# A Fourier-mixing layer with a gated MLP: x added by accumulating stores, three weight pairs split earlier, and the first two units of each MLP2 block interleaved

## The chip, the cores and the metric

The kernel runs on one core of one Trainium2 chip. The metric is the device time of one execution in microseconds (us). Several executions of the same program are timed, and their median is given. Beside that stands one execution that a profiler recorded; its rows are what the profile shows. Engines are named as in the profile: PE is the matrix engine (TensorE), DVE the vector engine, ACT the scalar engine, POOL is GpSimd, and SP is the engine that mainly issues transfers.

## What is computed

For x of 2048 tokens by 512 features, all in float32:

```python
xn = layernorm(x)                       # over the 512 features
a = xn @ dft_hid_re.T;  b = xn @ dft_hid_im.T
s = dft_seq_re @ a - dft_seq_im @ b     # real part of the 2D Fourier transform
h = relu(xn @ w1 + b1) ** 2             # w1: 512 x 1792
g = silu(h @ w2 + b2)                   # w2: 1792 x 512
out = x + s * g
```

## The kernel before, in words

**Arithmetic.** Every float32 operand is split into a high part (ACT, L69) and a low part (DVE, L72), both of type float32r, and each product of two operands is made of three passes: high x high, high x low, low x high. On top of that, products of 2 x 2 blocks are made by the Strassen-Winograd scheme with seven products instead of eight. So each operand first needs four *sums* (`sums_a`, `sums_b`, on DVE), and its seven pieces are then split. The seven results are put together by `combine` (L234): one copy by ACT and four DVE operations (L240 to L243) that read the PSUM banks.

**Stages.** (1) The sequence transform comes first, in eight blocks c of 256 columns with eight steps j each. Blocks 0 and 1 are computed plainly, blocks 2 to 7 by Strassen-Winograd (`mm`, L300). For each step a raw tile of the DFT matrix (`r`, 512 KB, L190, three slots) is loaded, its sums are formed (`t`, two slots) and it is split into two sets of moving operands, two steps ahead of use. `stage2` (L287) multiplies the result by the hidden-dimension DFT matrices and stores s as `Y` in memory. During this stage DVE and ACT also prepare the weight pairs (`make_w`): all seven of w1, and of w2 those that are not made later; they are stored in memory as `W1D` and `W2D`.
(2) MLP1 (`hidden`, L526) has 28 *units*, one for each of four token blocks c and seven weight pairs p, n = 7c + p. A unit is 42 matmuls. Its result is combined, goes through ReLU and square on ACT, and is stored in memory (`HD`, L558) by a transfer that ACT issues. The tile for it (`room`, L522) is one of three `r` slots or a fourth one, by n % 4.
(3) MLP2 has 28 units in the same numbering. Unit n reads `HD` back (`operand`, L561): load (SP, L570), sums (DVE, L207 to L209), split (ACT L69, DVE L72) into one of three places of `block`. A unit is 42 matmuls (`outer`, L599), which add up over the seven pairs of a block in seven PSUM regions. Before a block's first products, ACT writes the bias b2 into three of these regions (`bias`, L592). At a block's end `combine` yields z, and `finish` (L622) makes silu(z) * s + x quarter by quarter, spread over units of the next block. Silu is ACT (L640), the product is DVE (`times`, L644), and the addition of x is either DVE (`plus`, L649, with x loaded by `load_fin`) or, for two quarters of blocks 0 and 1, a transfer by GpSimd that adds x from memory onto z in SBUF (L632); `put` then stores those quarters. The last block is finished by a sequence of its own (from L846), with its last three units taken product by product (`rest`).

**What sets the order.** MLP1 and MLP2 stand under `manual_schedule`: each engine runs its instructions in the order of the program text, which a Python loop writes. `go(names)` advances a named job by one step: `h5` is operand 5 (load, sums, split), `x3` a half of the tokens of a block, `m1` its mean and scale, `w6` a late weight pair (`late_w2`), `l5` the load of a prepared pair from `W2D`. In unit n of MLP2 the loop issues the matmuls, then `h{n+3}` (sums), at a block's end the combine, then `h{n+2}` (split) and `h{n+6}` (load). `plan` puts jobs beside the units of MLP1. SP, ACT and POOL issue transfers in program order too, and wait in that order: a transfer whose source or destination isn't ready holds up what is issued behind it.

**Weight pairs of w2.** W2_LATE (4, 5) are split during MLP1 and stored in W2D. W2_DIRECT (0, 1, 6) are split straight into the place that they are used from: 0 and 1 in the last third of MLP1, and 6 in the first four units of MLP2.

**Order of products.** ORDER is 1, 2, 6, 7, 5, 3, 4. A block's first unit takes FIRST, 1, 2, 6, 4, 7, 5, 3; that of the last block FIRST_LAST. Products 2, 6 are in one pair of banks (m26), 7, 5, 3 in a group of three (m753), 1 and 4 in a bank each.

Of the kernel before, what the change touches and what calls it, by code (L numbers as in the profile page):

```python
# [12 lines left out]
P = 128  # L13
# [15 lines left out]
W2_LATE, W2_DIRECT = (4, 5), (0, 1, 6)  # L29
# [22 lines left out]
FIRST = (1, 2, 6, 4, 7, 5, 3)  # L52
# [10 lines left out]
def fnet_gated_kernel(ctx, tc, x, xt, ct, wd, w1, w2, b1, b2, out):  # L63
# [30 lines left out]

    def bcast(src, n):
        return bass.AP(tensor=src.tensor, offset=src.offset, ap=[[0, P], [1, n]])
# [10 lines left out]
    for tag, n in (("g0a", 1536), ("g1a", 2048), ("g0b", 1536), ("g1b", 2048)):  # L107
        buf(tag, [P, n], f"place_{tag}")
    b1s = pool.tile([P, NF], F32, name="b1s")
# [57 lines left out]
    def sums(g):  # L167


        s = xn32[ND * g, "tile"].rearrange("p j h (b n) -> p j (h b) n", b=2)  # L170
        t = s1[g] = buf("t", [P, ND, CW], f"s1_{g}", bufs=2)
        nc.vector.tensor_tensor(t, s[:, :, 1], s[:, :, 3], op=ALU.subtract)
        nc.vector.tensor_tensor(s[:, :, 1], s[:, :, 1], s[:, :, 0], op=ALU.subtract)
        nc.vector.tensor_tensor(s[:, :, 0], t, s[:, :, 0], op=ALU.subtract)
        return nc.vector.tensor_tensor(s[:, :, 2], s[:, :, 2], s[:, :, 0], op=ALU.add)
# [10 lines left out]
    def load_c(c, j, hs=slice(0, 2)):  # L186
        if (c, j) not in raw:
            raw[c, j] = buf("r", [P, 4, CW], f"r{c}_{j}", bufs=3)
        q = slice(2 * hs.start, 2 * hs.stop)
        nc.sync.dma_start(raw[c, j][:, q], ct[c, j, :, q])  # L190
# [22 lines left out]
    def moving(key, r):  # L213

        k = "ab"[turn[0] % 2]
        turn[0] += 1
        g0 = buf(f"g0{k}", [P, 2, 3, CW], f"g0_{key}", F32R)
        g1 = buf(f"g1{k}", [P, 2, 4, CW], f"g1_{key}", F32R)
        t = buf("t", [P, 4, CW], f"t_{key}", bufs=2)
        sums_b(t, r)  # L220
        split(g0[:, HI], g0[:, LO], r[:, I11:I21 + 1])
        split(g1[:, HI], g1[:, LO], t)
        return g0, g1
# [45 lines left out]
    def stage2(c, t, tag="bc"):  # L269
# [24 lines left out]
        nc.sync.dma_start(Y[n // TC][n % TC:n % TC + P], y)  # L294
# [227 lines left out]
    def room(n, name):  # L522

        return buf("r" if n % 4 < 3 else "sx", [P, 4, 256], name, bufs=3 if n % 4 < 3 else 1)

    def hidden(n, c, p):  # L526
# [31 lines left out]
        nc.scalar.dma_start(HD[c, p], x_)  # L558
        yield

    def operand(n, c, p):  # L561

        if n % 4 in (0, 3):
            tag, bufs = (("t", 2), ("r", 3))[n % 4 // 3]
            x_ = buf(tag, [P, 4, 256], f"hr{c}_{p}", bufs=bufs)
            e = None
        else:
            e = buf("e" if n == 2 else "g1" + "ab"[n % 4 - 1], [P, 8, 256], f"hr{c}_{p}")
            x_ = e[:, 4:8]
        nc.sync.dma_start(x_, HD[c, p])  # L570
        yield
        if e is None:
            t = buf(tag, [P, 4, 256], f"hs{c}_{p}", bufs=bufs)
            parts = (slice(0, 4), t), (slice(4, 7), x_[:, 0:3])
        else:
            t = e[:, 0:4]
            parts = (slice(0, 7), e[:, 0:7]),
        sums_a(t, x_[:, C12:C12 + 1], x_[:, C11:C22 + 1], x_[:, C11], x_[:, C21])
        yield
        g = ready[c, p] = sixth(2 + n % 3, 2)  # L580
        for s, src in parts:
            split(g[:, HI, s], g[:, LO, s], src)
        yield
# [27 lines left out]
    def load_fin(c):  # L611

        fin[c] = []
        for n, src in enumerate((Y[c], x[c * TC:(c + 1) * TC])):
            for m in range(2 if n == 0 or c > NTC - 3 else 1):
# [6 lines left out]
    def finish(c, e, k):  # L622

        if len(fin[c]) > 2 + k // 2:
            silu(e, k)
            times(c, e, k)
            plus(c, e, k)
            return
        silu(e, k)
        times(c, e, k)  # L630
        z = e[:, k].rearrange("p (k e) -> p k e", e=256)
        nc.gpsimd.dma_start(z, at(x[c * TC:(c + 1) * TC], k), accum_op=ALU.add)  # L632

    def put(c, e, k):
        nc.sync.dma_start(at(out[c * TC:(c + 1) * TC], k), e[:, k].rearrange("p (k e) -> p k e", e=256))
# [31 lines left out]
    for c, j in steps:  # L667
# [11 lines left out]
        if j in (1, 2):  # L679
            stage2(c - 1, j - 1)  # L680
# [8 lines left out]
        if c == NC - 1:  # L689
# [4 lines left out]
            if j in (2, 4):  # L694
                first = xt_half(0, j // 2 - 1, lambda k: e[:, 4:8] if (j, k) == (2, "r") else
                                buf(k, [P, 4, 256], f"x{k}0", bufs=3 if k == "r" else 2))
                next(first)
            if j in (3, 6):
                list(first)
            if j > 2:  # L700
# [33 lines left out]
    for c in range(NTC - 1):  # L734
# [5 lines left out]
        else:  # L740
            plan(c, 0, [], [f"m{c + 1}", q0, q1])
# [4 lines left out]
        if c < len(W2_LATE):  # L746
            w = f"w{W2_LATE[c]}"
# [15 lines left out]
    with ordered:  # L763
        before = None
        for n, (c, p) in enumerate(units):
# [4 lines left out]
            if n == 0:  # L770
                load_w1(5)
                load_w1(6)
            if n == len(units) - 1:
# [16 lines left out]
        for n, (c, p) in enumerate(units):  # L790
# [31 lines left out]
            go(*{0: ("l5",), 1: ("w6",)}.get(n, ()))  # L822
            if not last or p < REST:
                for k in ORDER if p else FIRST_LAST if last else FIRST:
# [4 lines left out]
            go(f"h{n + 3}")  # L829
# [4 lines left out]
            if c and not last and p in (3, 4):  # L834
                put(*done, p - 1)
            go(f"h{n + 2}", *{2: ("w6",), 3: ("w6",)}.get(n, ()), f"h{n + 6}")
# [4 lines left out]
            elif c:  # L841
                for k in ((2, 3), (0,), (1,), (), (), (), ())[p] if not last else ((), (0,), (1, 2), (3,), (), (), ())[p]:
# [93 lines left out]
```

## Time and profile before

| | |
|---|---|
| median of 3 runs | 707.34 us (707.24 to 708.02) |
| the profiled execution: time, and its span | 709.52 us, 707.7 us |
| DVE busy, MLP1 from 500 to 555 us | 50.70 of 55 us |
| DVE busy, MLP2 from 596 to 630 us | 32.44 of 34 us |
| all transfers in the span | 141.09 MB, mean 199 GB/s |
| largest rate in one fortieth of the span (548 to 566 us) | 398 GB/s |
| last matmuls start, end of the span | 699.49 us, 707.7 us |

A row of a timeline gives the start and the duration in us, the engine, the line of the kernel, the operation, output and inputs, and in square brackets the idle time of the engine before it and what ended that. A row of the waits gives who waited for whom, the total in us, how often, and the longest. A row of the transfers gives the destination and source, the engine whose queue issued it (SPq, ACTq, POOLq), the count, the size and the median time in us from issue to landing. A row of the windows gives for a stretch of the span the busy time of PE, PEld, DVE, ACT and POOL, then the granted PE clock (1.00 is full), the share of the DMA engines and GB/s.

### The profile page before, as it was taken

The numbers are of one execution on the slowest core, as the hardware profiler recorded it, in microseconds if no ns is written. First come the engines' busy times: TensorE is split into PE (matmuls) and PEld (weight loads), VectorE is DVE, ScalarE is ACT, GpSimd is POOL, SyncE is SP. The second block draws the span as 40 slices with busy tenths as digits, with TensorE's granted clock in tenths as the row PEclk, the third lists the DMA queues.
The fourth block names the chain that finished last, engine by engine and source line by source line (L and its number), as shares of the span: only waits on it lengthen the run. The fifth ranks groups of instructions, "written<-read, shape, count | busy, mean of one in ns | idle before, by whom it ended". The sixth has DMA issues, their size and how long they took to land.

```text
span 707.7 us, 12794 instructions
## 1 busy us (share of the span) xinstructions
PE 687.7 (97%) x5179; PEld 648.4 (92%) x5179; DVE 584.0 (83%) x886; ACT 346.6 (49%) x475; POOL 5.2 (1%) x8
## 2 busy tenths in 40 slices
PE   8999999999999999999999999999999898999985
PEld 5778788999999999999999989899999898999985
DVE  7999654779598798797797746999999789999885
ACT  4437332444353544544453324777777745454431
POOL 0000000000000000000000000000000000101000
PEclk9999999999999999999999999999999999999998
DMA  8622441534563653835836966665627975767652
GB/s 331 219 90 90 139 144 45 207 109 146 200 219 134 237 195 123 302 116 192 280 110 240 381 266 208 209 253 208 253 121 248 398 287 198 188 206 207 234 160 79
DMA packets 55306, 141.09 MB, mean 199 GB/s; under 512 B 5072, under 2 KB 21968, under 8 KB 53968
## 3 DMA queue, kind: packets, MB, share of 16 engines
q1 hardware_dynamic: 50128, 124.56, 50.9%
q10 hardware_dynamic: 4032, 14.68, 5.2%
q0 software_dynamic: 1088, 1.05, 1.0%
q8 instruction: 40, 0.66, 0.4%
q14 instruction: 18, 0.15, 0.1%
HBM read 97.00 MB, written 43.27 MB: 198 GB/s over the span
## 4 chain that ended last, share of the span: by engine, by line
PE 73%; DVE 17%; DMA 5%; issue 2%; ACT 1%; SPq 0%; DVEq 0%; ACTq 0%
PE m_b L300 23%; PE yps L287 12%; PE hps L545 7%; PE m_b_o L599 7%; PE m_bb L300 5%; PE m_ba L300 5%; DVE block L72 4%; PE hps_b L545 4%; PE pq_b L353 3%; PE hps_ba L545 2%; DVE g L72 2%; DMA hr<-hd 2%; DMA w2raw<-in_w 1%; PE m_bc_o L599 1%; DVE bn L133 1%
## 5 line engine op out<-in xcount | busy, mean ns | idle before, releaser
L300 PE MATMUL m_b<-g,block 128*128 128x256 f32 x1080 | 129.0, 276 | 0.0
L300 PEld LDWEIGHTS m_b<-g,block 128*128 128x128 f32 x1080 | 125.5, 188 | 0.0
L69 ACT ACTIVATE g<-r 128x768 fp32r<-128x768 f32 (+2 forms) x65 | 57.3, 884 | 83.5 <-PE m_b L300 38.3
L72 DVE TENSOR_TENSOR g<-r,g 128x768 fp32r<-128x768 f32 (+2 forms) x65 | 65.4, 1007 | 35.1 <-ACT g L69 34.7
L287 PE MATMUL yps<-wd,pq 128*128 128x512 f32 (+1 forms) x414 | 92.9, 374 | 0.0
L287 PEld LDWEIGHTS yps<-wd,pq 128*128 128x128 f32 x414 | 74.8, 188 | 14.0
L72 DVE TENSOR_TENSOR g<-t,g 128x1024 fp32r<-128x1024 f32 x48 | 58.6, 1222 | 10.6 <-ACT g L69 10.6
L545 PE MATMUL hps<-xT,block 128*128 128x256 f32 x504 | 60.1, 278 | 1.6 <-DVE h L243 1.4
L545 PEld LDWEIGHTS hps<-xT,block 128*128 128x128 f32 x504 | 58.7, 188 | 2.0 <-issue 1.5
L69 ACT ACTIVATE g<-t 128x1024 fp32r<-128x1024 f32 x48 | 50.3, 1048 | 13.2 <-PE m_ba L300 6.5
L353 PE MATMUL pq_b<-g,block 128*128 128x512 f32 x180 | 47.6, 398 | 1.8 <-DVE g L72 1.7
L599 PE MATMUL m_b_o<-w,block 128*128 128x256 f32 x360 | 44.2, 279 | 4.1 <-ACT m_b_o L592 4.1
L599 PEld LDWEIGHTS m_b_o<-w,block 128*128 128x128 f32 x360 | 42.4, 188 | 4.8 <-ACT m_b_o L592 4.7
L556 ACT ACTIVATE h<-h,b1s 128x512 f32<-128x512 f32 x56 | 37.3, 715 | 17.7 <-DVE h L242 17.4
L300 PE MATMUL m_b<-g,xc 128*128 128x256 f32 x360 | 45.1, 277 | 0.0
L69 ACT ACTIVATE block<-hr 128x768 fp32r<-128x768 f32 (+1 forms) x28 | 35.5, 1268 | 18.8 <-DVE hr L209 6.0
L72 DVE TENSOR_TENSOR block<-hr,block 128x768 fp32r<-128x768 f32 (+1 forms) x28 | 41.6, 1485 | 2.3 <-ACT block L69 2.3
L353 PEld LDWEIGHTS pq_b<-g,block 128*128 128x128 f32 x180 | 33.0, 188 | 11.3 <-DVE g L72 2.4
L300 PEld LDWEIGHTS m_b<-g,xc 128*128 128x128 f32 x360 | 42.9, 188 | 0.3
L201 DVE TENSOR_TENSOR t<-r 128x512 f32<-128x512 f32 x48 | 32.8, 684 | 5.5 <-DMA r<-in_ct 5.3
L545 PE MATMUL hps_b<-xT,block 128*128 128x256 f32 x288 | 35.0, 278 | 0.0
L545 PEld LDWEIGHTS hps_b<-xT,block 128*128 128x128 f32 x288 | 33.9, 188 | 0.0
(200 smaller groups left out, 1184.2 us busy)
## 6 DMA issues: line engine op xcount, KB each, us to landing
r<-in_ct SPq DMA_DIRECT2D x63, 512.0 KB, 3.6
hd<-h ACTq DMA_DIRECT2D x28, 512.0 KB, 4.4
hr<-hd SPq DMA_DIRECT2D x28, 512.0 KB, 4.8
w1d<-w0g SPq DMA_DIRECT2D x21, 512.0 KB, 3.3
block<-w1d SPq DMA_DIRECT2D x6, 1792.0 KB, 8.8
y<-ysb SPq DMA_DIRECT2D x16, 256.0 KB, 3.1
fin<-y SPq DMA_DIRECT2D x16, 256.0 KB, 4.8
out<-z SPq DMA_DIRECT2D x15, 256.0 KB, 3.5
```

What stands on the lines that cost most here:

```text
L69: nc.scalar.activation(hi, src, AF.Copy)
L72: return nc.vector.tensor_tensor(lo, src, hi.bitcast(F32), op=ALU.subtract)
L133: nc.vector.bn_stats(bn, t[:, h])
L201: nc.vector.tensor_tensor(t[:, 0:2], r[:, 0:1].to_broadcast([P, 2, 256]), r[:, 1:3], op=ALU.add)
L287: nc.tensor.matmul(ps[:, s], PQ[c, m, k // 2][:, a_, w:w + P], WD[m, k][:, b_, s], start=n == 0, stop=n > len(todo) - 3, skip_group_check= ...
L300: nc.tensor.matmul(ps[:, d * CW:(d + 1) * CW], w[:, a_, d * P:(d + 1) * P], mv(b_), start=first and d == 0 and (a_, b_) == (HI, HI), stop= ...
L353: nc.tensor.matmul(accs[c][k], w, g[:, b_, 2 * h:2 * h + 2], start=j == 0 and h == 0 and (a_, b_) == (HI, HI), stop=j == NJ - 1 and h == 1 ...
L545: nc.tensor.matmul(product(ms, k), W1[p][a][:, a_, q * P:(q + 1) * P], xT[c, q][:, b_, b], start=share not in first, stop=q == 1 and (a_, ...
L556: nc.scalar.activation(x_[:, s], x_[:, s], AF.Relu, bias=b1s[:, f:f + 1])
L599: nc.tensor.matmul(m[:, k * 256:(k + 1) * 256], g[:, a_, a, k * P:(k + 1) * P], W2[p][:, b_, b], start=p == 0 and k == 0 and (a_, b_) == ( ...
```

## The change

- **x by accumulating stores.** During blocks 2, 3 and 4 of the first stage SP copies the first three quarters of x into `out`, memory to memory, 1 MB each, right behind a store of `Y`. For blocks 0 to 2 of MLP2 `finish` now makes silu(z) * s, and GpSimd stores it into `out` with an accumulating transfer. `plus`, `put` and the loads of x remain for the last block alone. The quarters are finished one unit apart.
- **Pairs 4, 5, 6 in MLP1.** Pair 6 is in W2_LATE. Pair 4 is split in MLP1's first unit, pair 5 where pair 4 was, pair 6 where pair 5 was. Unit 1 of MLP2 loads pair 6 from W2D.
- **Interleaving.** In blocks 0 to 2 of MLP2, PE does some products of unit 0 and of unit 1 (1 and 4; in block 0 also 2 and 6), and then the rest of unit 0 and the rest of unit 1. At a block's end and start the split `h{n+2}` is issued ahead of the combine and of the sums `h{n+3}`.
- **Four stores by GpSimd.** The results of the last four units of MLP1 (n = 24 to 27) are stored by GpSimd, not by ACT.
- **Slots.** The `r` and `t` slots are cut from two larger tiles. Operands with n % 4 = 0 take both `t` slots as one piece, those with n % 4 = 3 the `r` slots 0 and 1, and are split by one instruction on each engine where there were two.

```diff
-W2_LATE, W2_DIRECT = (4, 5), (0, 1, 6)
+W2_LATE, W2_DIRECT = (4, 5, 6), (0, 1)
...
-FIRST = (1, 2, 6, 4, 7, 5, 3)
 FIRST_LAST = (1, 2, 5, 4, 6, 7, 3)
...
+    shared, turns, kept = {}, {"t": 0, "r": 0}, set()
+    def slot(tag, n):
+        return shared[tag][:, 4 * n:4 * n + 4]
+    def turn_of(tag, keep=False):
+        while True:
+            n = turns[tag]
+            turns[tag] = (n + 1) % {"t": 2, "r": 3}[tag]
+            if (tag, n) not in kept:
+                break
+        if keep:
+            kept.add((tag, n))
+        return slot(tag, n)
...
+    shared["r"] = pool.tile([P, 12, 256], F32, name="raws")
+    shared["t"] = pool.tile([P, 8, 256], F32, name="sums")
...
-        return buf("r" if n % 4 < 3 else "sx", [P, 4, 256], name, bufs=3 if n % 4 < 3 else 1)
+        return slot("r", n % 4) if n % 4 < 3 else buf("sx", [P, 4, 256], name)
...
-        nc.scalar.dma_start(HD[c, p], x_)
+        (nc.scalar if n < 24 else nc.gpsimd).dma_start(HD[c, p], x_)
...
+        e = shared["t"] if n % 4 == 0 else shared["r"][:, 0:8] if n % 4 == 3 else \
+            buf("e" if n == 2 else "g1" + "ab"[n % 4 - 1], [P, 8, 256], f"hr{c}_{p}")
+        x_, t = e[:, 4:8], e[:, 0:4]
         nc.sync.dma_start(x_, HD[c, p])
...
-        for s, src in parts:
-            split(g[:, HI, s], g[:, LO, s], src)
+        split(g[:, HI], g[:, LO], e[:, 0:7])
...
     def finish(c, e, k):
-        if len(fin[c]) > 2 + k // 2:
-            silu(e, k)
-            times(c, e, k)
-            plus(c, e, k)
-            return
         silu(e, k)
         times(c, e, k)
         z = e[:, k].rearrange("p (k e) -> p k e", e=256)
-        nc.gpsimd.dma_start(z, at(x[c * TC:(c + 1) * TC], k), accum_op=ALU.add)
-    def put(c, e, k):
-        nc.sync.dma_start(at(out[c * TC:(c + 1) * TC], k), e[:, k].rearrange("p (k e) -> p k e", e=256))
+        nc.gpsimd.dma_start(at(out[c * TC:(c + 1) * TC], k), z, accum_op=ALU.add)
...
-            stage2(c - 1, j - 1)
+            y_stored = stage2(c - 1, j - 1)
+        if PLAIN <= c < PLAIN + NTC - 1 and j == 2:
+            part_ = slice((c - PLAIN) * TC, (c - PLAIN + 1) * TC)
+            with tc.issue_after(y_stored.ins):
+                nc.sync.dma_start(out[part_], x[part_])
...
-            plan(c, 0, [], [f"m{c + 1}", q0, q1])
+            plan(c, 0, [], [f"m{c + 1}", q0, q1] + [f"w{W2_LATE[0]}"] * 3)
...
-        if c < len(W2_LATE):
-            w = f"w{W2_LATE[c]}"
+        if c < len(W2_LATE) - 1:
+            w = f"w{W2_LATE[c + 1]}"
...
                 load_w1(6)
+                go(f"w{W2_LATE[0]}")
...
-            go(*{0: ("l5",), 1: ("w6",)}.get(n, ()))
-            if not last or p < REST:
-                for k in ORDER if p else FIRST_LAST if last else FIRST:
+            go(*{0: ("l5",), 1: ("l6",)}.get(n, ()))
+            if last:
+                if p < REST:
+                    for k in ORDER if p else FIRST_LAST:
+                        add(k, p)
+            elif p < 2:
+                early = (1, 4) if c else (1, 2, 6, 4)
+                for k in early:
+                    add(k, p)
+                for f in (0, 1) if p else ():
+                    for k in ORDER:
+                        if k not in early:
+                            add(k, f)
+            else:
+                for k in ORDER:
                     add(k, p)
...
-            go(f"h{n + 3}")
+            passage = not last and p == NP - 1 or c and p == 0
+            go(f"h{n + 2}" if passage else f"h{n + 3}")
...
-            if c and not last and p in (3, 4):
-                put(*done, p - 1)
-            go(f"h{n + 2}", *{2: ("w6",), 3: ("w6",)}.get(n, ()), f"h{n + 6}")
+            go(f"h{n + 3}" if passage else f"h{n + 2}", f"h{n + 6}")
...
-                for k in ((2, 3), (0,), (1,), (), (), (), ())[p] if not last else ((), (0,), (1, 2), (3,), (), (), ())[p]:
+                for k in ((), (2,), (3,), (0,), (1,), (), ())[p] if not last else ((), (0,), (1, 2), (3,), (), (), ())[p]:
                     finish(*done, k)
```

More of the change, by code (lines that the diff above doesn't have):

```diff
@@ L170, in sums @@
         s = xn32[ND * g, "tile"].rearrange("p j h (b n) -> p j (h b) n", b=2)
-        t = s1[g] = buf("t", [P, ND, CW], f"s1_{g}", bufs=2)
+        t = s1[g] = turn_of("t")
         nc.vector.tensor_tensor(t, s[:, :, 1], s[:, :, 3], op=ALU.subtract)
@@ L187, in load_c @@
         if (c, j) not in raw:
-            raw[c, j] = buf("r", [P, 4, CW], f"r{c}_{j}", bufs=3)
+            raw[c, j] = turn_of("r")
         q = slice(2 * hs.start, 2 * hs.stop)
@@ L218, in moving @@
         g1 = buf(f"g1{k}", [P, 2, 4, CW], f"g1_{key}", F32R)
-        t = buf("t", [P, 4, CW], f"t_{key}", bufs=2)
+        t = turn_of("t")
         sums_b(t, r)
@@ L293, in stage2 @@
         n = (2 * c + t) * P
-        nc.sync.dma_start(Y[n // TC][n % TC:n % TC + P], y)
+        return nc.sync.dma_start(Y[n // TC][n % TC:n % TC + P], y)
     def mm(ps, w, mv, first, last):
@@ L557, in hidden @@
         nc.scalar.activation(x_, x_, AF.Square)
-        nc.scalar.dma_start(HD[c, p], x_)
+        (nc.scalar if n < 24 else nc.gpsimd).dma_start(HD[c, p], x_)
         yield
     def operand(n, c, p):
[L563 to L569, printed above, removed]
+        e = shared["t"] if n % 4 == 0 else shared["r"][:, 0:8] if n % 4 == 3 else \
+            buf("e" if n == 2 else "g1" + "ab"[n % 4 - 1], [P, 8, 256], f"hr{c}_{p}")
+        x_, t = e[:, 4:8], e[:, 0:4]
         nc.sync.dma_start(x_, HD[c, p])
         yield
[L572 to L577, printed above, removed]
         sums_a(t, x_[:, C12:C12 + 1], x_[:, C11:C22 + 1], x_[:, C11], x_[:, C21])
@@ L613, in load_fin @@
         fin[c] = []
-        for n, src in enumerate((Y[c], x[c * TC:(c + 1) * TC])):
-            for m in range(2 if n == 0 or c > NTC - 3 else 1):
+        for n, src in enumerate((Y[c], x[c * TC:(c + 1) * TC])[:1 + (c == NTC - 1)]):
+            for m in range(2):
                 tag = f"pq{n}{m}" if c < NTC - 1 else (("g0a", "sx"), ("g0b", "pq10"))[n][m]
@@ L695, in fnet_gated_kernel @@
                 first = xt_half(0, j // 2 - 1, lambda k: e[:, 4:8] if (j, k) == (2, "r") else
-                                buf(k, [P, 4, 256], f"x{k}0", bufs=3 if k == "r" else 2))
+                                turn_of(k, True))
                 next(first)
@@ L699, in fnet_gated_kernel @@
                 list(first)
+                kept.clear()
             if j > 2:
```

## The prediction, made before the changed kernel was run

> **What bounds the kernel now.** I read the page first, then the waits of PE, then PE's timeline through MLP2, then DVE, ACT and SP where a wait pointed at them.
>
> ```profile
> span 707.7 us, 12794 instructions
> ...
> PE 687.7 (97%) x5179; PEld 648.4 (92%) x5179; DVE 584.0 (83%) x886; ACT 346.6 (49%) x475; POOL 5.2 (1%) x8
> ```
>
> PE is busy for 97% of the span, so a change that leaves its matmuls as they are (this one does) can only win back idle time or a longer pace. Which engine PE waits for, in total, times, longest:
>
> ```profile
> PE m_b_o L599 <- ACT m_b_o L592: 4.1, 3, 2.5
> PE m L599 <- DVE block L72: 2.3, 1, 2.3
> ...
> PE hps L545 <- DVE h L243: 1.4, 1, 1.4
> ...
> PE m_bb_o L599 <- DVE block L72: 0.5, 2, 0.4
> ```
>
> Three of the four are in MLP2 (L599): for a bank's bias, and for the split of an operand. PE's timeline shows what they cost. Units of MLP2 start at these rows:
>
> ```profile
> 554.97 0.84 PE L599 MATMUL m_bb_o<-w,block 128*128 128x256 f32 x6
> ...
> 560.38 2.33 PE L599 MATMUL m_b_o<-w,block 128*128 128x256 f32 x18 [2.53 <-ACT m_b_o L592]
> ...
> 567.30 0.84 PE L599 MATMUL m_bb_o<-block 128*128 128x256 f32 x6
> ...
> 581.58 0.39 PE L599 MATMUL m_bb_o<-w,block 128*128 128x256 f32 x2
> ...
> 592.18 0.84 PE L599 MATMUL m_bc_o<-w,block 128*128 128x256 f32 x6
> ...
> 599.14 0.84 PE L599 MATMUL m_bc_o<-w,block 128*128 128x256 f32 x6
> ...
> 637.63 0.87 PE L599 MATMUL m_bc_o<-block 128*128 128x256 f32 x6
> ...
> 642.58 0.87 PE L599 MATMUL m_bc_o<-block 128*128 128x256 f32 x6
> ...
> 682.34 0.39 PE L599 MATMUL m<-w,block 128*128 128x256 f32 x2
> 685.07 0.78 PE L599 MATMUL m<-w,block 128*128 128x256 f32 x4 [2.33 <-DVE block L72]
> 685.65 1.48 PE L599 MATMUL m<-block 128*128 128x256 f32 x6
> ...
> 689.29 2.88 PE L599 MATMUL m<-w,block 128*128 128x256 f32 x24
> ```
>
> Units 2, 3 and 4 take 581.58 - 567.30 = 14.28, or 4.76 us a unit of 42 matmuls, 0.1134 each. Against that, in excess:
> - units 0 and 1: 567.30 - 554.97 - 9.52 = **2.81** (bias of m753, held by MLP1's last combine);
> - units 5 and 6: 592.18 - 581.58 - 9.52 = **1.08** (splits behind the late weight pair 6 on DVE);
> - unit 7, first of block 1: 599.14 - 592.18 - 4.76 = **2.20** (banks of block 0);
> - in the last block, 685.07 - 682.34 - 0.23 = **2.5** of waiting, then 18 matmuls in 689.29 - 685.65 = 3.64 instead of 2.04: **1.6** at a lower clock.
>
> Sum 10.2. A unit of block 2 takes 642.58 - 637.63 = 4.95, with no wait marked: seven such are 1.3 us.
>
> The lower clock has its own row (granted clock after POOL's time):
>
> ```profile
> 686.00:687.00 1.00, 1.00 (x7) 1.00 (x6) 1.00 (x2) 0.00 (x0) 0.00 (x0) 0.50 1.03 335
> ```
>
> Here a wait of 2.33 us was followed by half clock; the 2.53 at 560.38 was not (18 matmuls in 2.33). So I count the 1.6 as lost with the wait. [...]
>
> **The change, part by part.**
>
> *Interleaving, start of MLP2.* PE does products 1, 2, 6, 4 of units 0 and 1 first, 48 matmuls: until 554.97 + 5.44 = 560.41. The bias for 5:
>
> ```profile
> 551.78 0.33 ACTq L558 DMA_DIRECT2D hd<-h  x1
> ...
> 559.29 0.33 ACTq L558 DMA_DIRECT2D hd<-h  x1
> 559.72 0.60 ACT L592 ACTIVATE m_b_o<-b2s 128x512 f32<-128x512 f32 x1 [2.18 <-DVE hr L208]
> ```
>
> It ends at 560.32, so it is in time even unmoved; and ACT idled for 2.18 around the store of a hidden unit at 559.29, which now goes to GpSimd. The 2.81 goes. What is late next is unit 2's operand, wanted at 554.97 + 9.52 + 0.23 = 564.7 (two matmuls need only the high part):
>
> ```profile
> 561.48 0.69 DVE L207 TENSOR_TENSOR hs<-hr 128x512 f32<-128x512 f32 x1 [1.48 <-DMA hr<-hd]
> ...
> 562.66 0.42 DVE L209 TENSOR_TENSOR hs<-hs,hr 128x256 f32<-128x256 f32 x1
> ...
> 564.82 2.03 DVE L72 TENSOR_TENSOR block<-hr,block 128x1792 fp32r<-128x1792 f32 x1 [1.73 <-ACT block L69]
> ```
>
> DVE does the sums of operand 3 first (561.48 to 563.08, 1.6 us, waiting for its load), then the low split of operand 2 (2.0). Operand 3's load changes place. It went to the slot of hidden unit 24; now it goes to slot 1, from which hidden unit 25 is stored, and that store is GpSimd's:
>
> ```profile
> 552.62 0.32 SPq L570 DMA_DIRECT2D hr<-hd  x1
> ```
> ```profile
> hd<-h ACTq DMA_DIRECT2D x28, 512.0 KB, 4.4
> hr<-hd SPq DMA_DIRECT2D x28, 512.0 KB, 4.8
> ```
> ```profile
> hd<-h ACTq DMA_DIRECT2D x5, 512.0 KB, 8.3
> ```
> ```profile
> 603.40 1.33 POOL L632 DMA_DIRECT2D z<-in_x  x1 [602.96 <-DVE z L644]
> ```
>
> (Third fence: the window 540 to 575 alone.) The store of unit 25 left ACT at 551.78; from POOL, whose one issue shown took 1.33, about 553.1. It lands 4.4 to 8.3 later, 557.5 to 561.4, and the load takes 4.8 to 8.9 (its own now, 552.62 to 561.48): 562.3 to 570.3. SP stands still meanwhile, with pair 4's load, operand 5's and those of pairs 5 and 6 behind it. So the transfers ahead drain and little shares the load: I take 6.3 and 4.8, landing 564.2. Low split done 564.2 + 1.6 + 2.0 = 567.8: PE waits **3.1** (1.2 to 9.2). The start is a swap, -2.81 + 3.1. Later loads (pair 4 is wanted by unit 4, 577 or later) were queued behind the same transfers before, so I add nothing for them.
>
> *Pair 6 in MLP1, units 5 and 6.* DVE loses pair 6's sums and low split here (1.6 + 2.0). The 1.08 goes; pair 6's copy from memory is 1.8 MB instead of 0.5, ahead of operand 7 on SP, and may give some back: 0 to 0.7, I take 0.2.
>
> *Block 0 to 1.* Block 1 now starts with products 1 and 4 of two units (24 matmuls, 2.72 us), in banks of their own, then 2 and 6 of unit 7: until 4.08 after block 0's end (592.18) nothing needs the bank that the combine's third step holds.
>
> ```profile
> 592.43 1.22 DVE L240 TENSOR_TENSOR z<-m_b_o,z 128x1024 f32<-128x1024 f32 x1
> ...
> 595.01 1.22 DVE L242 TENSOR_TENSOR z<-m_b_o,z 128x1024 f32<-128x1024 f32 x1
> ```
>
> That step ended 596.23 - 592.18 = 4.05 after it. Unit 8's split now goes ahead of the combine and unit 9's sums behind it: 2.0 - 1.6 = 0.4 later, but pair 6's 3.6 is gone from the work ahead. So 2.20 becomes 0 to 0.7; 0.2 taken. Block 1 to 2 has nothing to lose. Block 2 to 3 has the swap without the interleaving: +0.5 (0 to 1).
>
> *x by accumulating stores.* DVE loses the additions at L649: two in block 1, two in block 2, four in the last block. The last block is where it counts:
>
> ```profile
> 679.54 0.69 DVE L649 TENSOR_TENSOR z<-z,fin 128x512 f32<-128x512 f32 x1
> ...
> 682.99 2.02 DVE L72 TENSOR_TENSOR block<-hr,block 128x1792 fp32r<-128x1792 f32 x1
> ```
>
> The split at 682.99 (operand 26) ends the 2.33 wait. Ahead of it go three additions (about 0.65 each with their issue, 1.9) and operand 22's low split, moved ahead of the combine (2.0); operand 23's sums come in (1.6). 685.0 - 2.3 = 682.7, wanted at 682.34 + 0.23 = 682.57: 2.5 + 1.6 become 0.2 (0 to 1; a short wait, no lower clock). POOL's 12 issues of 1.33 lie beside everything; no instruction waits for them.
>
> The three copies of x, 1 MB each, go through SP in blocks 2 to 4 of the first stage, ahead of raw loads:
>
> ```profile
> r<-in_ct SPq DMA_DIRECT2D x63, 512.0 KB, 3.6
> ...
> block<-w1d SPq DMA_DIRECT2D x6, 1792.0 KB, 8.8
> ```
>
> A raw tile's slot is refilled some two steps (9.5 us) ahead of its use. A copy priced by bytes read, 8.8 / 1.79 = 4.9, makes 8.5: hidden; priced by read and write, 3.6 + 8.8 = 12.4, it costs up to 2.9 each. I take 0: operands are also split two steps ahead.
>
> *Pair 4's split in MLP1's unit 0.* DVE and ACT are idle there, but on ACT it stands ahead of the copies of the two last DFT tiles, and unit 1 needs the bank of the first.
>
> ```profile
> 423.06 4.92 PE L545 MATMUL hps<-xT,block 128*128 128x256 f32 x42
> ```
> ```profile
> 408.25 0.56 SPq L486 DMA_DIRECT2D w1b<-w1d  x1
> ```
> ```profile
> w1b<-w1d SPq DMA_DIRECT2D x1, 1024.0 KB, 12.7
> ```
>
> The raw weights queue behind w1b (408.25 + 12.7 = 421.0), so land at 421 to 424.6 (plus 3.6). Sums 1.6, high split about 1 to 2, copy 0.6: unit 1 starts at about 424.5 or later, not 423.06, 1.4 to 5 late. The 1.4 wait for h L243 comes after it and absorbs as much: 0 to 3.5, I take **0.5**. Pairs 5 and 6 take the places that 4 and 5 had, so the later blocks keep their load. The merged splits of every fourth and its neighbour's operand and the tiles cut as slices are costed at nothing: same bytes, fewer instructions on DVE and ACT.
>
> **Sum**: 0.5 + (3.1 - 2.81) + (0.2 - 1.08) + (0.2 - 2.20) + 0.5 + (0.2 - 4.1) = -5.5. The profiled execution took 709.52 with its 707.7 span, so 704.0; the median of three runs was 707.34, so **701.8**.
>
> **Rivals.**
> - *Longer pace.* The 4.95 pace of block 2 begins and ends at short waits, so which waits remain may choose it. Two more blocks at 4.95: 14 x 0.19 = +2.7, **704.5**. Block 2 back at 4.76: -1.3, and with operand 3 at its earliest -1.9 more: **698.6**. For: it comes without a marked cause. Against: most of MLP2 ran at 4.76.
> - *The last wait stays.* Something else than DVE's queue holds operand 26: -5.5 + 3.9 = -1.6, **705.7**. Against: no wait is marked on that split.
> - *Slower: GpSimd's store holds SP.* If unit 25's store starts late or lands late, operand 3, then pairs 4 to 6 and operands 5 to 7 come late, and PE waits for one after the other. From a landing of operand 3 at 564.2 + 5.5 = 569.7 all is lost; at the upper ends, 570.3, the result is 707.9, and another 3 us of starting late give **710.9**. For: DVE is busy without a break there. Against: the POOL issue at 603.40 took 1.33 beside a busy DVE. [...]
>
> **Numbers.** Forecast 0.55 (its own range 699 to 704.5); longer pace 0.12; shorter pace and early operand 0.08; last wait stays 0.12; slower 0.13. Faster by over 0.2% (1.4 us, about what a measurement of this kernel can tell from no change) takes the forecast, both paces and half of the last wait: 0.80; within, the other half and the mild part of the slower case: 0.10; slower 0.10. Range 697.5 to 706.5.
>
> **What would show it.** Right: no wait on L592 after 554.97; one wait of 1 to 4 us for operand 2's split at unit 2; SP's load of operand 3 issued after 557; no half clock near 686; unit 1 of MLP1 1 to 3 us later. Wrong: units 3 to 7 waiting on loads, waits at L300, a wait near 682, or 4.95 us units where none were.

## The result, and the profile after

The changed kernel takes **715.27 us** (median of 4, 713.25 to 718.24); the kernel before took 707.68 beside it (median of 4, 707.24 to 708.91). The ratio is 1.0106, 95% interval 1.0080 to 1.0133. The prediction gave 701.8 with 706.5 as its upper end, so the sign was wrong: 7.6 us slower, not 5.5 faster. Two of the executions timed for the experiments, one of the kernel before and one of a variant, took about two and three and a half times as long as the rest, and the ratios leave them out.

The profiled execution took 713.25 with a span of 711.5, 3.8 more than the span of before. It lies 2.0 below its kernel's median, and that of before 1.8 above, so the two spans show only half of the difference. The account below is between the spans; the other half comes at the end of the reasons.

The page and PE's waits:

```profile
span 711.5 us, 12744 instructions
...
PE 690.4 (97%) x5179; PEld 651.9 (92%) x5179; DVE 578.4 (81%) x865; ACT 345.4 (49%) x462; POOL 16.9 (2%) x20
```
```profile
PE m L605 <- ACT m L598: 4.3, 1, 4.3
PE m_bb_o L605 <- DVE block L71: 4.0, 1, 4.0
...
PE hps L562 <- ACT ysb L309: 1.3, 1, 1.3
...
PE m L605 <- DVE block L71: 0.4, 1, 0.4
```

L605 is `outer`, L598 the bias, L71 the low split, L562 MLP1's matmuls, L309 the copy at the end of `stage2`. The bias waits at the starts of MLP2 and of block 1 are gone, and the wait for operand 26 fell from 2.3 to 0.4. In their place stand two waits that are longer than any of before. PE's timeline at the same places as before:

```profile
424.64 3.57 PE L562 MATMUL hps<-xT,block 128*128 128x256 f32 x28 [1.29 <-ACT ysb L309]
...
554.38 0.84 PE L605 MATMUL m_bb_o<-w,block 128*128 128x256 f32 x6
...
568.27 0.74 PE L605 MATMUL m_bb_o<-block 128*128 128x256 f32 x4 [3.98 <-DVE block L71]
568.85 5.20 PE L605 MATMUL m_b_o<-block 128*128 128x256 f32 x30
...
574.60 0.87 PE L605 MATMUL m_bb_o<-block 128*128 128x256 f32 x6
...
594.39 0.87 PE L605 MATMUL m_bc_o<-w,block 128*128 128x256 f32 x6
...
604.28 0.87 PE L605 MATMUL m_bc_o<-block 128*128 128x256 f32 x6
...
663.00 0.87 PE L605 MATMUL m_ba_o<-w,block 128*128 128x256 f32 x6
668.16 2.74 PE L605 MATMUL m<-w,block 128*128 128x256 f32 x12 [4.29 <-ACT m L598]
...
674.65 2.88 PE L605 MATMUL m<-w,block 128*128 128x256 f32 x24
...
690.37 0.74 PE L605 MATMUL m<-w,block 128*128 128x256 f32 x4 [0.37 <-DVE block L71]
...
703.66 0.87 PE L605 MATMUL m<-w,block 128*128 128x256 f32 x6
```

Units 0, 3, 7, 9, 21 and 22 of MLP2 start at 554.38, 574.60, 594.39, 604.28, 668.16 and 674.65; the wait at 568.27 is in unit 2.

Rows of before that complete the comparison (the starts of units 3, 9, 21 and 22 of MLP2):

```profile
572.06 0.84 PE L599 MATMUL m_bb_o<-block 128*128 128x256 f32 x6
...
603.90 0.84 PE L599 MATMUL m_bc_o<-block 128*128 128x256 f32 x6
...
662.36 1.58 PE L599 MATMUL m<-w,block 128*128 128x256 f32 x12
...
667.38 2.88 PE L599 MATMUL m<-w,block 128*128 128x256 f32 x24
```

| stretch | before | after | difference | forecast |
|---|---|---|---|---|
| to MLP2's start | 554.97 | 554.38 | -0.6 | +0.5 |
| units 0 to 2 | 17.09 | 20.22 | **+3.1** | +0.3 |
| units 3 to 6 (up to block 1) | 20.12 | 19.79 | -0.3 | -0.9 |
| units 7 and 8 | 11.72 | 9.89 | -1.8 | -2.0 |
| units 9 to 20 | 58.46 | 59.4 | +1.0 | 0 |
| unit 21, first of the last block | 5.02 | 10.9 | **+5.9** | +0.5 |
| from there to the last matmuls | 32.11 | 29.01 | -3.1 | -3.9 |

With -0.4 behind the last matmuls this adds up to the 3.8. Two lines carry the loss; in units 3 to 20 the difference to the forecast comes from a longer pace of PE, 4.95 us a unit instead of 4.76 (see the rivals). Both long waits were followed by half clock, in the windows view:

```profile
569.00:570.00 1.00, 1.00 (x9) 1.00 (x8) 0.96 (x3) 0.18 (x1) 0.00 (x0) 0.71 0.89 365
...
668.00:669.00 1.00, 0.84 (x5) 0.84 (x6) 0.97 (x2) 0.10 (x1) 0.00 (x0) 0.70 0.70 287
```

Each time the clock stayed at one half for 3.413 us (the trace's clock records). At the first place 30 matmuls took 574.60 - 568.85 - 0.70 = 5.05 instead of 3.40.

**What unit 2 waited for.** The chain of waits, then DVE:

```profile
551.00 9.37 DMA hd<-raws
...
560.50 4.08 DMA raws<-hd
```
```profile
564.67 0.69 DVE L224 TENSOR_TENSOR raws<-raws 128x512 f32<-128x512 f32 x1 [5.92 <-DMA raws<-hd]
...
566.20 2.02 DVE L71 TENSOR_TENSOR block<-hr,block 128x1792 fp32r<-128x1792 f32 x1
```

Unit 25's store by GpSimd left at 551.00 and landed 9.37 later. Only then could operand 3's load go into its slot, and DVE stood at operand 3's sums with operand 2's split behind them: the forecast's mechanism (landing 564.2 forecast, 564.6 measured).

**What unit 21 waited for.** ACT, then POOL:

```profile
665.62 0.60 ACT L256 ACTIVATE z<-m_bc_o 128x512 f32<-128x512 f32 x1 [5.02 <-DMA out<-z]
```
```profile
645.02 1.19 POOL L633 DMA_DIRECT2D out<-z  x1 [20.29 <-DVE z L642]
649.82 1.18 POOL L633 DMA_DIRECT2D out<-z  x1 [3.61 <-DVE sums L225]
654.57 1.19 POOL L633 DMA_DIRECT2D out<-z  x1 [3.57 <-DVE hr L226]
659.38 1.19 POOL L633 DMA_DIRECT2D out<-z  x1 [3.61 <-issue]
```

`combine` at the end of block 2 writes z into the tile with the tag `e`, the only one. Block 1's four quarters sit in it until their accumulating stores have landed, and the last one was issued at 659.38 and landed 6.13 later, as the chain of waits has it:

```profile
659.38 6.13 DMA out<-z
```

Block 2 was done at about 663.7 (663.00 and six matmuls).

Each of the three stores before it landed 4.4 to 4.5 us after it left, and the next one left 0.3 behind that. So it is in all nine places of this kernel where one of these stores follows another. The profile names no releaser for it (the row at 659.38 says issue), so this is read from the times; whether the program or the queue makes the store wait is not shown. In the kernel before, the last store out of this tile left at 648.42 and landed 5.8 later, 8 us ahead of block 2's end:

```profile
648.42 0.41 SPq L635 DMA_DIRECT2D out<-z  x1
```

### The profile page after: what moved, and what is told of

Same layout as the page of the kernel before. It is cut to its first block, busy times and chain, and to the rows that moved or that the text cites. A ratio compares the mean times of both kernels' runs of the same rounds, so it can differ in the third digit from the quotient of the medians.

```text
span 711.5 us, 12744 instructions
## 1 busy us (share of the span) xinstructions
PE 690.4 (97%) x5179; PEld 651.9 (92%) x5179; DVE 578.4 (81%) x865; ACT 345.4 (49%) x462; POOL 16.9 (2%) x20
## 4 chain that ended last, share of the span: by engine, by line
PE 68%; DVE 15%; issue 7%; DMA 6%; ACT 1%; POOL 1%; SPq 0%; DVEq 0%; ACTq 0%; POOLq 0%
PE m_b L317 23%; PE yps L304 11%; PE hps L562 9%; PE hps_b L562 5%; PE m_bb L317 5%; PE m_ba L317 4%; DVE block L71 3%; PE pq_b L370 3%; PE m_b_o L605 3%; PE hps_ba L562 2%; DVE g L71 2%; DMA hd<-raws 1%; DMA w2raw<-in_w 1%; PE hps_bb L562 1%; DVE bn L150 1%
## 5 line engine op out<-in xcount | busy, mean ns | idle before, releaser
L68 ACT ACTIVATE g<-raws 128x768 fp32r<-128x768 f32 (+2 forms) x65 | 57.4, 885 | 92.7 <-PE m_b L317 41.6
L71 DVE TENSOR_TENSOR g<-raws,g 128x768 fp32r<-128x768 f32 (+2 forms) x65 | 65.3, 1006 | 33.2 <-ACT g L68 33.0
L71 DVE TENSOR_TENSOR g<-sums,g 128x1024 fp32r<-128x1024 f32 x48 | 58.6, 1221 | 10.0 <-ACT g L68 10.0
L562 PE MATMUL hps<-xT,block 128*128 128x256 f32 x504 | 59.7, 278 | 1.3 <-ACT ysb L309 1.3
L562 PEld LDWEIGHTS hps<-xT,block 128*128 128x128 f32 x504 | 58.6, 188 | 1.6 <-ACT ysb L309 1.6
L68 ACT ACTIVATE g<-sums 128x1024 fp32r<-128x1024 f32 x48 | 50.3, 1048 | 14.6 <-PE m_ba L317 7.8
L605 PE MATMUL m_b_o<-w,block 128*128 128x256 f32 x360 | 43.9, 280 | 0.0
L605 PEld LDWEIGHTS m_b_o<-w,block 128*128 128x128 f32 x360 | 42.9, 189 | 0.0
L218 DVE TENSOR_TENSOR sums<-raws 128x512 f32<-128x512 f32 x49 | 33.6, 686 | 8.7 <-DMA raws<-in_ct 8.5
L68 ACT ACTIVATE block<-hr 128x1792 fp32r<-128x1792 f32 x14 | 23.8, 1700 | 25.7 <-DVE hr L226 12.8
L562 PE MATMUL hps_b<-xT,block 128*128 128x256 f32 x288 | 34.9, 277 | 0.0
L605 PE MATMUL m_b_o<-block 128*128 128x256 f32 x270 | 34.8, 289 | 0.0
L605 PEld LDWEIGHTS m_b_o<-block 128*128 128x128 f32 x270 | 34.0, 197 | 0.0
L562 PEld LDWEIGHTS hps_b<-xT,block 128*128 128x128 f32 x288 | 33.8, 188 | 0.0
```

Of the source, the lines that this page charges most:

```text
L68: nc.scalar.activation(hi, src, AF.Copy)
L71: return nc.vector.tensor_tensor(lo, src, hi.bitcast(F32), op=ALU.subtract)
L218: nc.vector.tensor_tensor(t[:, 0:2], r[:, 0:1].to_broadcast([P, 2, 256]), r[:, 1:3], op=ALU.add)
L562: nc.tensor.matmul(product(ms, k), W1[p][a][:, a_, q * P:(q + 1) * P], xT[c, q][:, b_, b], start=share not in first, stop=q == 1 and (a_, ...
L605: nc.tensor.matmul(m[:, k * 256:(k + 1) * 256], g[:, a_, a, k * P:(k + 1) * P], W2[p][:, b_, b], start=p == 0 and k == 0 and (a_, b_) == ( ...
```

## The experiments

**Theory T**: the loss is that tile, held by stores that follow one another, and operand 3's load; each costs its wait and a half clock behind it. **R1**: block 2's sums are late because finishing is spread over more units. **R3**: TensorE's longer pace (4.95 us a unit instead of 4.76) carries it. Each ratio is to the kernel before on the same chip, with its 95% interval; waits are from one profiled execution. The changed kernel stands at 1.0106. All edits are to it.

### Tiles for block 1's sums

```diff
-                e = buf("e", [P, 4, 512], f"z{c}")
-                combine(e, ms)
+                if c == 1:
+                    e = Two(*(buf(f"pq1{i}", [P, 2, 512], f"z{c}_{i}") for i in range(2)))
+                    combine_two(e, ms)
+                else:
+                    e = buf("e", [P, 4, 512], f"z{c}")
+                    combine(e, ms)
```

`combine_two` makes the same sums by seven operations, as the two tiles don't lie side by side.

> The sums of block 1 go to two tiles that are idle in MLP2 instead of the one tile that all blocks share, so block 2's sums need not wait for block 1's four accumulating stores. Theory T (the single tile, held by stores that GpSimd issues one after another about 4.8 us apart, ends last at blocks 2 to 3): ScalarE's copy at the end of block 2 no longer waits 5 us, TensorE's wait of 4.3 us for the bias goes, and the half clock at 668.4 with it; the span is 4.5 + 1.8 = about 6 us shorter, 705 to 706 us. Rival R1 (the sums of block 2 are late because the finishing work is spread over more units and VectorE is behind): the wait stays within 1 us of 4.3 us and the time within 1 us. Rival R3 (the longer pace of TensorE explains the loss): the wait goes, yet the time falls by less than 3 us.

709.2, ratio 1.0042 (1.0027 to 1.0058); span 707.1, 4.4 less. Unit 21 waits 0.60 instead of 4.29 and runs at full clock. Its stretch fell from 10.9 to 5.7. R1 falls: the finishing steps stood where they were. R3's bound (less than 3 us) is not met, but the span alone doesn't rule R3 out: operand 26's wait came back, 1.91, and the clock was at one half twice as long behind unit 2 (6.827 us), some 3 us lost, while the longer pace held for 55 us of MLP1 and MLP2 instead of 132, some 3 us won.

### Operand 3 in another slot; ScalarE's stores; both homes

```diff
+        if n == 3:
+            x_, t = slot("r", 0), slot("r", 1)
```

Slot 0 is unit 24's; what follows (sums, split in two parts) is as for this operand before.

> Operand 3 is read into the slot of hidden unit 24 instead of that of unit 25, with its sums in the other slot and its split in two parts. T (the start of MLP2 lost its gain because this load waits for unit 25's store by GpSimd, issued at 551.0 and landed 9.4 us later): the load goes out between 553 and 557 instead of at 560.5, TensorE's wait of 4.0 us in unit 2 goes or falls below 1 us, and the half clock at 569.4 (1.6 us) goes: 4 to 5.6 us less. Rival (VectorE is the bound there, whatever the slot): the wait stays above 2.5 us and the gain is below 2 us.

712.94, ratio 1.0091 (1.0069 to 1.0113), not told apart from 1.0106. The load went out at 557.51, later than expected; unit 2 waits 2.38, with a half clock. And what was won turned up one block on: a wait of 2.15 at the start of block 2 and 2.05 at that of the last, both for the tile `e`. Neither expectation was met.

```diff
-        (nc.scalar if n < 24 else nc.gpsimd).dma_start(HD[c, p], x_)
+        nc.scalar.dma_start(HD[c, p], x_)
```

> The last four stores of hidden units are issued by ScalarE again; the slots stay those of the changed kernel. T with the slow store as the cause: unit 25's store lands in about 4 to 5 us instead of 9.4, operand 3's load goes out at about 556, the 4.0 us wait and its half clock go: 3 to 5.6 us less. If only the choice of the slot matters and not who stores: the load still goes out after 559 and the wait stays above 2 us. If ScalarE's own issues take the place of the wait, the first operands of MLP2 come later and the gain is below 2 us.

714.48, ratio 1.0122 (1.0099 to 1.0145). The store issued by ScalarE was nearly as slow as GpSimd's:

```profile
551.13 7.91 DMA hd<-raws
...
559.18 4.29 DMA raws<-hd
```

The same store took 7.2 from ScalarE in the kernel before, and 7.3 to 9.4 in the 14 profiled executions that have it on GpSimd. So who issues it matters little, and T's part about GpSimd falls in the main. Unit 2 still waits 2.39.

> Both edits: block 1's sums in tiles of their own, and operand 3 in unit 24's slot. T: both waits and both half clocks go, 6 + 4 to 5.6 = 10 to 11.6 us less than the changed kernel, a span of about 700 to 702 us, 5 to 8 us below the kernel before. R3 (pace): the waits go, but the time stays within 3 us of the kernel before.

The edits of the first two together: 708.13, ratio 1.0026 (1.0008 to 1.0044). Unit 21 waits 0.91, unit 2 still 1.61: the load went out at 553.50, but its data came only at 562.8, 9.3 us later, and DVE stood before it again. 5.7 us less in the medians, where 10 to 11.6 were expected.

### The order on VectorE at unit 0

```diff
-            passage = not last and p == NP - 1 or c and p == 0
+            passage = not last and p == NP - 1 or p == 0
```

> One word of the order by hand: at unit 0 of MLP2, too, operand 2's split stands ahead of operand 3's sums, as the change has it at the other blocks' starts. T (the wait in unit 2 comes from VectorE standing in front of sums whose operand has not landed, with a finished operand behind it): the 4.0 us wait goes and so does the half clock behind it, though operand 3 lands as late as before (564 to 565); unit 3 then waits at most 1 us. Unit 2 ends 4 to 5.6 us earlier; the span falls by 3 to 5.6 us, less what block 1's and 2's sums then wait longer for the shared tile. Rival (the load itself is the bound): the wait moves to unit 3 and stays above 2 us.

714.92, ratio 1.0107 (1.0087 to 1.0127). Unit 2 has no wait any more and unit 3 waits 0.31, so the order was the cause there: unit 3 starts at 569.85, 4.75 us earlier. Nothing of it reaches the end. By the end of block 2 only 0.2 was left, since other waits had taken it up (1.28 at unit 6, 0.98 at block 1, 1.75 at the start of block 2 for the tile `e`). And the last block starts when the tile is free, here 1.8 later than in the changed kernel, as block 1's last store took 6.9 us to land (why longer is not shown):

```profile
669.92 2.93 PE L605 MATMUL m<-w,block 128*128 128x256 f32 x12 [6.30 <-ACT m L598]
```

### Finishing at the earlier units

```diff
-  ((), (2,), (3,), (0,), (1,), (), ())[p] if not last
+  ((2, 3), (0,), (1,), (), (), (), ())[p] if not last
```

> The finishing steps at the units of the kernel before (two quarters at the block's first unit, then one each), still with accumulating stores into the one tile's place. T (the four stores follow one another, about 4.8 us apart, and their last one must have landed before the tile can be written): all four move about 5 us ahead, the last lands at about 656 to 661, and block 2's wait of 4.3 us falls below 1 us, with its half clock: 4 to 6 us less. Rival (VectorE and ScalarE are then crowded at the blocks' starts, which the spreading avoided): waits for operands of 1 us and more appear in the first three units of blocks 2 and 3, and the gain is below 3 us.

708.91, ratio 1.0031 (1.0014 to 1.0047), 5.3 us less than the changed kernel, as T has it. Unit 21 waits 0.80. POOL shows that the stores follow one another even where their data is ready: DVE had both first quarters by 640.5.

```profile
640.29 1.19 POOL L633 DMA_DIRECT2D out<-z  x1 [18.82 <-DVE z L642]
644.82 1.18 POOL L633 DMA_DIRECT2D out<-z  x1 [3.34 <-DVE z L642]
649.80 1.19 POOL L633 DMA_DIRECT2D out<-z  x1 [3.80 <-DVE sums L225]
654.48 1.19 POOL L633 DMA_DIRECT2D out<-z  x1 [3.49 <-DVE hr L226]
```

The rival's crowding is there too, but small: 0.9 at the fourth units of blocks 1 and 2.

### Without the accumulating stores

`finish`, `put`, `load_fin` and the units of finishing as before, no copies of x.

> The whole change except the accumulating stores: finishing, the loads of x and the stores as in the kernel before, no copies of x into the output. T: without stores that must land one after another the shared tile comes free in time, and block 2's wait of 4.3 us and its half clock go, 4 to 6 us less, as with tiles of their own. What the accumulating stores were worth shows in the last block: if they were what shortened operand 26's wait from 2.33 to 0.37 us, that wait comes back at 1.5 us or more. Rival: the sums are late for another reason, the wait stays above 3 us.

713.77, ratio 1.0102 (1.0084 to 1.0121). Unit 21 waits 0.88, as T has it, and yet nothing is won. The last block's wait came back, longer than before, and with it half clock (from 690.20 six matmuls took 1.28 instead of 0.68); MLP1's unit 1 also had half clock in this execution, 6.67 for its 42 matmuls where the kernel before took 4.92:

```profile
689.46 0.94 PE L605 MATMUL m<-w,block 128*128 128x256 f32 x4 [3.42 <-DVE block L71]
```
```profile
425.55 6.67 PE L562 MATMUL hps<-xT,block 128*128 128x256 f32 x42 [2.38 <-ACT ysb L309]
```

### Weight pair 4 behind the copies

Unit 1 of MLP1 waits for ACT, which stands at pair 4's split, whose raw weights landed late, while the copies that free unit 1's bank queue behind it. In the changed kernel:

```profile
421.39 0.85 ACT L68 ACTIVATE w2g0a<-w2raw 128x768 fp32r<-128x768 f32 x1 [9.87 <-DMA w2raw<-in_w]
...
424.01 1.06 ACT L309 ACTIVATE ysb<-yps 128x512 f32<-128x512 f32 x2
```

```diff
-            plan(c, 0, [], [f"m{c + 1}", q0, q1] + [f"w{W2_LATE[0]}"] * 3)
+            plan(c, 0, [], [f"m{c + 1}", q0, q1] + [f"w{W2_LATE[0]}"])
...
                 stage2(NC - 1, 1, "ba")
+                go(*[f"w{W2_LATE[0]}"] * 2)
```

> Of the three edits only the one in MLP1: the split and stores of weight pair 4 stand behind ScalarE's copies of stage 2's last products, all else as changed. T: unit 1 of MLP1 starts at 423.1 to 423.4 instead of 424.6, and since nothing behind it has slack, the whole program is 1.3 to 3 us shorter. Rival (the later waits, for stores and loads, take it up): less than 0.5 us.

715.62, ratio 1.0128 (1.0109 to 1.0148). Unit 1 starts at 423.22 without a wait. The rival holds, and shows why the changed kernel resists: block 2 is done some 3 us earlier, and its wait is twice as long.

```profile
670.47 2.93 PE L605 MATMUL m<-w,block 128*128 128x256 f32 x12 [9.60 <-ACT m L598]
```
```profile
653.08 1.19 POOL L633 DMA_DIRECT2D out<-z  x1 [4.20 <-issue]
659.64 1.19 POOL L633 DMA_DIRECT2D out<-z  x1 [5.37 <-issue]
```

Block 1's third store landed at 659.3, after 6.2 us, and the fourth at 667.83, after 8.2. The loads of Y for the next finishing left SP at 658.35, now ahead of the fourth store; in the changed kernel they left at 660.63, behind it. That these transfers slow the store is my reading; no run takes them away alone.

### Three edits together, and one undone at a time

Own tiles for block 1's sums, the order at unit 0, and pair 4 behind the copies:

> Three edits together: block 1's sums in tiles of their own, operand 2's split ahead of operand 3's sums at unit 0, and the split and stores of weight pair 4 in MLP1's unit 0 behind ScalarE's copies of the last two products of stage 2. T: the waits of 4.3 and 4.0 us and both half clocks go, and MLP1's unit 1 waits below 0.3 us instead of 1.3 to 2.6: 10 to 14 us less than the changed kernel, and 2 to 6 us below the kernel before, which is what the prediction gave the change. Rival R3 (TensorE's longer pace, taken up by chance at each restart, decides): the waits go, but the time stays within 2 us of the kernel before, with the longer pace over 60 us or more.

**705.45, ratio 0.9975 (0.9961 to 0.9988)**: faster than the kernel before, and than the changed one by 1.3%, 9.3 us. Span 702.4. Both are a little less than T's 2 to 6 and 10 to 14 us. The time lies within 2 us of the kernel before, as R3 has it, but R3's reason is missing: the longer pace held for 27 us, not for 60.

```profile
PE m_bb_o L621 <- DVE block L71: 2.1, 2, 1.8
...
PE m L621 <- DVE block L71: 1.2, 1, 1.2
...
PE m L621 <- ACT m L614: 0.9, 1, 0.9
```

The same without new tiles, with finishing at the earlier units instead:

> The three causes mended without a new tile: finishing at the units of the kernel before, operand 2's split first at unit 0, weight pair 4 split behind the copies. T: all long waits go, as in the run with three edits, so 704 to 707 us, at or below the kernel before. Rival (the earlier finishing crowds VectorE): waits for operands of 1 to 2 us at the second unit behind a block's start, and 2 to 4 us more than the run with three edits.

707.33, ratio 1.0011 (0.9999 to 1.0022): not told from the kernel before and 2.5 us more than the three edits, as its rival has it. Waits of 0.93 and 1.02 in the fourth units of blocks 1 and 2, 1.85 at unit 5.

What is each part of the change worth, once nothing holds it back? The five runs that follow undo one part each; all but the fourth start from the three edits.

> The run with three edits, but the products of a block's first two units are not interleaved (order of the kernel before). The prediction gave the interleaving 2.81 us at MLP2's start, 1.08 in units 4 and 5 behind it and 2.20 at blocks 0 to 1. T: these waits (2.5 for the bias at MLP2's start, 1.3 and 0.3 at blocks 0 to 1) come back, 3 to 6 us more, so 708 to 711 us. Rival (the interleaving only moves the wait to the next operand): less than 1.5 us.

The line for p < 2 is replaced by `for k in ORDER if p else FIRST`. 708.42, ratio 1.0028 (1.0013 to 1.0043), 3.7 us more: the bias waits are back, 0.72 at MLP2's start, 0.84 and 0.33 at block 1, 0.24 and 0.39 at block 2. Of the 2.81 at MLP2's start only 0.72 came back.

> The run with three edits, but with the last four stores of hidden units issued by ScalarE. If GpSimd's issuing is worth something there: 4 issues of 0.33 us plus about 0.46 us of waiting behind each come back on ScalarE, 1 to 3 us more. If the stores' issuer makes no difference, as without the edits: within 1 us.

705.52, ratio 0.9988 (0.9973 to 1.0003): the intervals overlap, so who issues the four stores is not told apart.

> Block 1's sums in their own tiles and operand 2's split first, with the weight pairs as in the kernel before: pairs 4 and 5 split in MLP1 a block later each, pair 6 split in MLP2's first units. If moving pair 6 ahead is worth something: VectorE and ScalarE carry 1.6 + 2.0 and 1.7 us more in units 1 to 3 of MLP2, waits there of 1 us and more, 2 to 4 us above the run with three edits. Rival (pair 6 lies beside other work in MLP2 too): within 1.5 us.

The weight pairs' plan as before, pair 6 split in MLP2 (and so no pair 4 in unit 0). 709.46, ratio 1.0052 (1.0037 to 1.0066), 5.4 us more, which is above the expected 2 to 4. DVE stands for pair 6's raw weights with the operands behind it, and unit 5 waits 4.06:

```profile
577.57 0.69 DVE L218 TENSOR_TENSOR w2raw<-w2raw 128x512 f32<-128x512 f32 x1 [4.37 <-DMA w2raw<-in_w]
```

> The two orders mended (operand 2's split first, weight pair 4 behind the copies), with finishing, loads of x and stores as in the kernel before: no accumulating stores, one tile. If the accumulating stores are worth something once they hold nobody up (T: four sums of 0.69 us less on VectorE ahead of operand 26's split): the last block's wait is 1.5 to 3.5 us with a half clock of 1.6 behind it, and the time 2 to 5 us above the run with three edits, 707 to 711 us. Rival (they are worth nothing, only their waits cost): within 1 us of the run with three edits.

711.06, ratio 1.0082 (1.0066 to 1.0099). Against the run with one tile (1.0011), which differs from it in the accumulating stores (and the copies of x) alone, they are worth 0.7%, 5 us: operand 26's wait is 4.09 without them and 1.91 with them. The profiled executions of the two held the longer pace for 90 and 27 us, worth some 2.5 us; how much of the 5 us that is in the medians no run shows.

> The run with three edits, and finishing at the units of the kernel before. If earlier stores still help (block 3's sums of the last block, the loads of the finishing data): 0.5 to 2 us less, below 705 us. If the spreading is right once no tile is held: 0.5 to 2 us more, with waits for operands at the second unit behind a block's start as in the run with one tile (0.9 and 1.0 us).

707.53, ratio 1.0021 (1.0011 to 1.0031): 3.2 us more than with the spread steps, with waits of 0.94 and 0.67 at the fourth units of blocks 1 and 2. The spreading is right once no tile is held.

## Why the prediction was wrong

**The step that failed** is "POOL's 12 issues of 1.33 lie beside everything; no instruction waits for them", and with it "Block 2 to 3 has the swap without the interleaving: +0.5 (0 to 1)". The issues do lie beside everything (1.2 each). What is waited for is their landing. In the kernel before SP stored the quarters, two behind DVE's additions in the block's first units and two by `put` in its fourth and fifth; the change gave all four to one queue in which each store went out 0.3 behind the landing of the one before (4.3 to 5.4 us apart), began a unit later, and left one tile. Most of what was needed was there: which tile the next combine writes, which transfer reads it last, and as the nearest row GpSimd's adding transfers of before (5.4 us to landing, the second of a block 0.3 behind the landing of the first). The forecast asked what an instruction of POOL costs and not what its transfer holds. It cost 5.9 us instead of 0.5, and the run with own tiles was 4.5 us faster (0.64% between the ratios). All the signs that the forecast named for being right came, and of those for being wrong only the 4.95 us units: its list had no sign for the tile.

**MLP2's start** was right in mechanism and missed by the half clock: 3.98 of wait instead of 3.1, and 1.65 behind it for which the sum had nothing. That operand 3's landing was met within 0.4 us is luck in part: the store left at 551.0 instead of 553.1, took 9.4 instead of 6.3 (8.3 at most), and the load behind it took 4.1 instead of 4.8. The forecast had seen that a wait of 2.33 was followed by half clock in the last block, and did not apply that to the 3.1 us wait that it forecast itself. The order on DVE, which it also named, was the cause to mend: one word removes the wait.

**Unit 1 of MLP1** started at 424.64 (forecast 424.5) and cost nothing in the profiled execution, since a later wait absorbed it. **Units 5 to 8** and **operand 26** went as forecast: 1.08, 2.20 and 2.33 became 0, 0 and 0.37. Of the 3.9 in the last block 3.1 came; its end ran at the longer pace (690.6 to 703.7). **The copies of x** cost nothing: no wait was added in the first stage.

**The rivals.** The longer pace came too, at about the price that its rival gave it: by the matmuls' pitch in the trace (118 ns instead of 113) it held for 132 us of MLP1 and MLP2 instead of 67, about 2.6 us more (65 x 0.04). That is a large part of the 3.8 between the spans, and what causes it is not shown. It doesn't decide: by the rival's own sum the kernel would still be faster, and the run with the order alone held it for about 29 us only and yet had a span of 713.2. The slower rival (GpSimd's store holds SP) gave the right sign for the wrong reason; its point, 569.7 for operand 3, was not reached.

**Why two of the mends gave nothing singly.** The waits are in series, and the tile is free at a time that doesn't follow PE. With pair 4 alone block 2 was done 3 us earlier, and the wait behind it grew from 4.29 to 9.60. With the order alone the gain went into waits ahead of block 2's end, and the tile came free later: 6.30. Each of the two alone measured nothing; beside own tiles they bring 0.67% together, 4.7 us (1.0042 to 0.9975).

**The other half of the 7.6.** The four executions of the changed kernel had spans and mean clocks of 711.5 at 0.994, 713.4 at 0.991, 716.5 at 0.986 and 713.6 at 0.992; those of the three edits ran from 701.9 to 705.3 at 0.996 to 0.999. One stretch of 3.413 us at half clock lowers the mean by 3.413 / 2 / 711 = 0.0024, and costs 1.7 us. From 0.994 to 0.986 are about three of them, 5 us, which is the spread. One of them is uncertain, since the mean also counts half clock behind the last matmuls, which costs nothing (2.1 us of it in the profiled execution, 5.1 in that of before). That the waits cause such stretches in some executions and not in others is argued from this and from the last section, not shown row by row.

**Still open.** With its waits mended the change is worth 0.25% (1.8 us), not 0.8%, although its profiled span (702.4) is 5.3 below that of before. The span of before on which the sum was built, 707.7, is a long one: on the four later chips all but one of that kernel's executions had spans of 702.6 to 707.6. Of the 5.3, some 1.6 is the pace (27 us at the longer one instead of 67). The 1.6 of half clock in its last block, which the sum counted as a sure gain, need not be in each execution; no run separates this.

## What to carry to other kernels

Price a transfer by what it holds until it has landed (here the tile it reads, the slot behind it, the next accumulating store of its queue: 6.13 us for the last store of block 1) and not only by the engine time of its issue (1.19): list for every buffer who writes it next. When a change moves work and the time doesn't follow, look for a wait that grew by what was won, and mend the waits together before judging any part. On each engine whose order the program fixes, ask whether something finished stands behind something that hasn't landed, as operand 2's split stood on DVE here (3.98 us of wait for PE).

## What the runs showed of the hardware

Half clock ahead of the last matmuls came in stretches of 3.413 us (one in the kernel before, two in the changed one) or whole multiples (6.827 in the run with own tiles, 10.240 in that with pair 4 later, behind the wait of 9.60). PE's waits of 1.76 (three edits, unit 5), 1.85 (one tile, unit 5; behind each of the two 30 matmuls took 5.18 instead of 3.56), 2.33 (the kernel before, last block) and 2.38 (operand 3 in another slot, unit 2) were followed by half clock, while 2.53 (the kernel before, start of MLP2) and 2.70 (without accumulating stores, unit 2) were not. From 419 us on all waits of 3 us and more were, from 3.08 (finishing at the earlier units, unit 2) to 9.60. What tells the shorter ones apart is not shown.

Hidden unit 25's store, 512 KB among the weight loads, took 7.3 to 9.4 us to land from GpSimd's queue and 7.2 to 8.1 from ScalarE's (the kernel before and the two runs in which ScalarE issues it).

An accumulating store of GpSimd, 256 KB, landed 4.0 to 8.2 us after it left, in half of the cases within 4.5, and the next one left 0.26 to 0.34 behind its landing each time. GpSimd's plain stores did not wait like this: the one at 551.00 left before the one of 546.57 had landed (551.68).
